# First routing's clearings behind the first gathers, warming matmuls and smaller blocks in it, and the networks' turns, low parts and builds in other slots

## The chip, the cores and the metric

One core of a Trainium2 chip runs the whole program. The metric is the device time of one execution in microseconds (us): 639.29 us is the median of three runs of the kernel before (638.78 to 642.51). The engines are TensorE (PE, matrix products), VectorE (DVE), ScalarE (ACT), GpSimd (POOL) and the transfer queues, of which SyncE's (SP) carries weights and clearings and POOL's the indirect gathers and scatters. Each engine works through its own instructions in order and waits on the others by semaphores.

## The reference

Three stages follow one another, on 24,576 rows (tokens) of 256 values:

```python
X = np.fft.fft(np.fft.fft(x, axis=1), axis=2).real          # x: 8 x 3072 x 256
# first mixture: E = 8 experts, F = 1024
P = np.exp(x @ w_gate - (x @ w_gate).max())
for _ in range(8):
    P /= P.sum(1, keepdims=True) + 1e-09
    P /= P.sum(0, keepdims=True) + 1e-09
    P *= N / E
out = sum(P[:, e:e + 1] * (np.maximum(x @ w1[e], 0) @ w2[e]) for e in range(E))
# second mixture: only the expert with the largest logit, times its softmax probability
expert_idx = np.argmax(logits, axis=1)
out2[mask_e] = gate_w[mask_e, None] * (np.maximum(x[mask_e] @ u1[e], 0) @ u2[e])
```

## The kernel before

The kernel computes the transform (`fft_phase`, to about 196 us), stores the half spectrum in a table `H` (a row and its mirror share an entry; even and odd parts lie side by side), and then works on the rows that carry weight. The **first routing** (`route1`, L575) finds those rows: it makes a list of 29 tiles of 128 slots (24 for the experts, CAP = 3 each, and NF1 = 5 free ones). The position of each row in the list comes out of one-hot matmuls. DVE builds blocks of one-hot columns `ah` (`rows`, L556) of the sizes in CH1 = (24, 24, 16), and PE multiplies each column with 58 columns of `bv` (`runs`, L568, the matmul in L572). From the sums in PSUM (`pt`) DVE makes the row numbers `Rhidx`, POOL gathers rows of `H` into `Xg` (`grab`, L1366, one indirect transfer per tile, with two small clearings of `grow` ahead of each from group 2 on), and a second small product, `bq` against the first block, gives positions in the accumulator. Meanwhile PE has matmuls for the gates of the second mixture (`gates2`, L1279); the string table G2 (L1497) says, one string for each of seven places in the routing, what is put there: "g" one gate piece of 16 matmuls, "0" to "3" low parts, "l" the load of `Ld`, "z" six clearings of the result (`zeros(2)`, 512 KB each from the zero tile `zt`) and the accumulator's clearing (L1348), "v" two warming matmuls on a zero tile `zb`. The clearings are issued on SP.

Each of the eight expert **networks** is computed with weights and activations split in two parts, high and low (`part`, L836: the high part on ACT, the low, `w1l`, `w2l`, on DVE in 1.22 us), three products per block: eight blocks of the first layer (L916, `ph`), `hh` by ACT (L902) and the low part `hl` by DVE (L438), and then the second layer (L949, `py`) in three tiles of slots. So PE waits for `hl` wherever DVE is occupied. Other work is hung into that order by hand. `Slots` has places (e, s) of expert e: s = 0 to 7 behind the first-layer blocks, 8 to 10 the free tile, 11 the turn, 12 to 20 in the second layer's three tiles. Tables say where it goes: PART low and high parts of the next expert's weights, BUILD and FBUILD the four steps in which a gathered group becomes input `x` (add, sign, add, subtract, in `build`, L1620), GRAB1 the gathers, LOGIT the logits of a group, PROB the probabilities of the second mixture, STEPS the eight Sinkhorn rounds. In a round the column sum goes through PE (L1022, `cs`) and ACT (L1023, `total`); the rest is a chain of small DVE operations (`turn`): scale the columns, sum the rows, reciprocal, scale, mask, column sum.

`route1` also returns `later`, the rest of the routing (the free tiles' expert, nine DVE operations: `nf` to `Rfrow`), which `moe1` runs at slot (0,4) in `begin`. The second routing and the second network (`route2`, `moe2`) are built alike; their `later` runs ahead of the second network.

Of the kernel before, what the change touches and what calls it, by code (L numbers as in the profile page):

```python
# [7 lines left out]
F32 = mybir.dt.float32  # L8
# [362 lines left out]
CH1, CH2 = (24, 24, 16), (10, 10, 9)  # L371
# [75 lines left out]
class Route:  # L447
# [9 lines left out]
    def positions(self, T, M, n, rst, nf_, hook=lambda: None, S=None, n1=None, between=()):  # L457
# [56 lines left out]
        def later():  # L514
# [5 lines left out]
            s1, s2 = R["sel"][:, :nf_], S([nf_, 8], name="s2_")  # L520
# [4 lines left out]
            ef = S([nf_], name="ef")  # L525
            o.red(ef, s2, ALU.add)
            wr = S([nf_], name="wr")
# [28 lines left out]
    def rows(self, pool, rb, a, n):  # L556
        m = self.K["irx"].shape[2]
        ah = pool(128 * m)[:, :128 * n].rearrange("p (r i) -> p r i", i=n)
        self.o.tt(ah, self.K["irx"][:, :, :n], rb[:, None, a:a + n].to_broadcast([128, 128, n]), ALU.is_equal)
        return ah  # L560
# [14 lines left out]
def route1(nc, rt, L, rmx, K, R, keep, pool, ring, hooks):  # L575
# [4 lines left out]
    S = lambda sh, dt=F32, name=None: keep.tile([128] + list(sh), dt, name=name)  # L580

# [77 lines left out]
    gp, later = rt.positions(T, M, NSA, C("rst"), NF1, during, S, NSL)  # L659
# [23 lines left out]
    eq, gq = T([8, NSL], name="eq"), T([8], name="gq")  # L683
    lst, li = S([2, NT1], name="lst"), T([NT1], I32, name="li")
# [10 lines left out]
    def signs():  # L695

        o.cp(lst, pv)
# [3 lines left out]
        o.ts(R["valid"], lst[:, 0], 0.5, ALU.is_ge)  # L701
        o.ts(sf, lst[:, 1], 127.5, ALU.is_ge)
        o.stt(R["prim"], sf, -1.0, R["valid"], ALU.mult, ALU.add)
        o.stt(R["ow"], R["hidx"], 2.0, sb, ALU.mult, ALU.add)

        o.tt(eq, ja[:, NSL:NSL + 8, None].to_broadcast([128, 8, NSL]), ja[:, None, :NSL].to_broadcast([128, 8, NSL]), ALU.is_equal)
        o.tt(eq, eq, gp[:, None, :NSL].to_broadcast([128, 8, NSL]), ALU.mult)
        o.red(gq, eq, ALU.add)
        tq, rq, _ = rt.split(T, gq, None, 8, "q")
# [11 lines left out]
        rt.more()  # L721
        pq = rt.py.tile([128, 512], F32, name="py")
        rt.runs(pq, late, bq, 0, 24, True, True)
        st["pq"] = pq

    def targets():

        lq = R["lq"]
# [22 lines left out]
def route2(nc, rt, lg, K, R, pool, ring, arrive, more, counts, warm):  # L751
# [3 lines left out]
    T = lambda sh, dt=F32, name=None: pool.tile([128] + list(sh), dt, name=name)  # L755
    mx, km, rk, kp = T([NT1], name="mx"), T([NT1], name="km"), T([NT1, 8], name="rk"), T([NT1], name="kp")
# [34 lines left out]
    gp, later = rt.positions(T, M, NT1, C("rst2"), NF2, during, between=at)  # L791
# [187 lines left out]
def sinkhorn(nc, K, R, pt, pool):  # L979
# [31 lines left out]
    def rows(it):  # L1011
# [3 lines left out]
        V.reciprocal(ri, rs)  # L1015
        o.tt(P, P, bc(ri), ALU.mult)
# [29 lines left out]
    for it in range(8):  # L1046
        steps += [turn(it), sums]
# [125 lines left out]
def run(tc, ctx, A, out, H, acc, Ld, Pd, Gd, Zd):  # L1173
# [19 lines left out]
    for nm, sh, dt in (("gm", [1], F32), ("ovf", [1], F32), ("sel", [max(NF1, NF2), 8], F32), ("hidx", [NT1], I32),  # L1193
                       ("sg", [NT1], F32), ("valid", [NT1], F32), ("prim", [NT1], F32), ("apos", [E], I32), ("oidx", [NF1], I32), ("lq", [2, E], F32),
# [41 lines left out]
    with tc.manual_schedule():  # L1236
# [27 lines left out]
        with ExitStack() as st:  # L1264
# [50 lines left out]
            with ExitStack() as s1:  # L1315
                r1 = P(s1, "r1", 1, side="right")
                r1a = P(s1, "r1a", 3, side="right")
                ring = lambda n: r1a.tile([128, n], BF16, name="ah")
# [13 lines left out]
                def fill(k):  # L1332

                    def f():
                        for c in G2[k]:
# [5 lines left out]
                            elif c == "z":  # L1341
                                for _ in range(6):
                                    zeros(2)
# [19 lines left out]
                signs, later = route1(nc, rt, L, rmx, K, R, S, r1, ring, [fill(i) for i in range(1, 5)] + [lambda: low(0, 1)])  # L1363
# [14 lines left out]
                for j in (0, 1):  # L1378
                    grab(j)
                fill(5)()  # L1380
                signs()
                fill(6)()
                assert not half
                warm(W2)
            with ExitStack() as s1:
# [4 lines left out]
                def rest():  # L1390
                    later[2]()
# [504 lines left out]
```

## Time and profile before

| what | value |
|---|---|
| median of three runs | 639.29 us |
| profiled execution, its time | 638.99 us |
| its span | 637.2 us |
| PE busy | 615.2 us (97%) |
| DVE busy | 435.4 us (68%) |
| ACT busy | 328.6 us (52%) |
| POOL busy | 194.1 us (30%) |

The span runs from the first to the last instruction; the execution's time holds 1.8 us more around it. Rows of a timeline give the start of a group of like instructions, how long the group takes, its engine and line, what it writes and reads, and in brackets the idle time ahead of it and what ended that. Where matmuls follow each other, their ends are modelled, so that rows of neighbours overlap. [...]

### The profile page before, as it was taken

What the parts mean: (1) busy time and instruction counts of PE and PEld (TensorE: products, weight loads), DVE (VectorE), ACT (ScalarE), POOL (GpSimd) and SP (SyncE); (2) the same over time, 40 slices, a digit from 0 to 9 for tenths busy, and PEclk for the clock granted to TensorE, in tenths of its full rate; (3) what the DMA queues carried; (4) which work ended last, traced back from release to release, by engine and by line L of the source; (5) the groups of instructions that cost most, each with busy time, mean ns of one, the idle gap of its engine ahead of it and who ended that gap; (6) DMA issues with size and microseconds to landing.
All of it is one profiled execution on the core that took longest, in us unless ns stands there. A gap on an engine that the chain in (4) does not pass through costs nothing. (4 is left out here: it accounts for less than half of the span.)

```text
span 637.2 us, 12627 instructions
## 1 busy us (share of the span) xinstructions
PE 615.2 (97%) x4778; PEld 593.4 (93%) x4783; DVE 435.4 (68%) x981; ACT 328.6 (52%) x756; POOL 194.1 (30%) x318
## 2 busy tenths in 40 slices
PE   9999999999999999999999999999999999999995
PEld 6889999999999998999899999986899999999995
DVE  3697877688346977759898796856755664754760
ACT  3455555555544504547566468642455564654551
POOL 0002201221011058871201101223785655422422
PEclk9999999999999958999999999999999999999998
DMA  8999999999998976787877989863655548436421
GB/s 211 284 247 273 275 274 285 279 264 296 341 338 246 414 274 223 221 304 258 281 238 289 338 299 239 196 179 61 224 181 190 197 160 308 184 137 275 175 83 38
DMA packets 56927, 152.56 MB, mean 239 GB/s; under 512 B 8307, under 2 KB 25851, under 8 KB 49436
## 3 DMA queue, kind: packets, MB, share of 16 engines
q1 hardware_dynamic: 47644, 114.69, 58.2%
q0 software_dynamic: 8752, 36.50, 16.8%
q8 instruction: 39, 0.64, 0.4%
q10 hardware_dynamic: 464, 0.51, 0.2%
q14 instruction: 28, 0.23, 0.1%
HBM read 101.50 MB, written 50.07 MB: 238 GB/s over the span
## 5 line engine op out<-in xcount | busy, mean ns | idle before, releaser
L438 DVE SCALAR_TENSOR_TENSOR hl<-ph,hh 128x384 fp32r<-128x384 f32 (+1 forms) x161 | 85.1, 543 | 78.0 <-ACT hh L902 77.8
L949 PE MATMUL py<-w2h,hh 128*128 128x256 f32 (+1 forms) x472 | 136.0, 288 | 0.9 <-ACT lg L1678 0.9
L949 PE MATMUL py<-w2h,hl 128*128 128x256 f32 (+1 forms) x472 | 133.7, 283 | 1.1 <-DVE hl L438 1.0
L949 PE MATMUL py<-w2l,hh 128*128 128x256 f32 (+1 forms) x472 | 133.1, 282 | 0.3 <-DVE w2l L854 0.3
L902 ACT ACTIVATE hh<-ph 128x384 fp32r<-128x384 f32 (+1 forms) x161 | 75.9, 481 | 57.4 <-PE ph L916 33.9
L949 PEld LDWEIGHTS py<-w2h,hl 128*128 128x128 f32 x472 | 88.8, 188 | 1.9 <-DVE hl L438 1.9
L949 PEld LDWEIGHTS py<-w2h,hh 128*128 128x128 f32 x472 | 88.9, 188 | 1.5 <-ACT lg L1678 1.3
L949 PEld LDWEIGHTS py<-w2l,hh 128*128 128x128 f32 x472 | 89.1, 189 | 0.5 <-DVE w2l L854 0.5
L916 PE MATMUL ph<-xh,w1h 128*128 128x384 f32 x256 | 68.2, 347 | 4.0 <-DVE hl L438 3.2
L916 PE MATMUL ph<-xh,w1l 128*128 128x384 f32 x256 | 65.8, 339 | 0.0
L916 PE MATMUL ph<-xl,w1h 128*128 128x384 f32 x256 | 65.6, 338 | 0.0
L823 POOL DMA_INDIRECT out_dram<-y,Rorow x30 | 34.8, 1159 | 86.4 <-ACT hh L902 43.7
L126 POOL TENSOR_TENSOR lc<-hd 128x32 f32<-128x32 f32 x23 | 9.0, 393 | 164.5 <-ACT hd L122 150.5
L74 PE MATMUL pp<-ca,w 96*128 96x96 f32 x512 | 59.0, 275 | 0.0
L74 PEld LDWEIGHTS pp<-ca,w 96*128 96x128 f32 x512 | 58.2, 192 | 0.5 <-ACT Z L97 0.2
L916 PEld LDWEIGHTS ph<-xh,w1h 128*128 128x128 f32 x256 | 45.4, 190 | 6.6 <-DVE hl L438 4.8
L84 DVE COPY t<-pp 128x512 f32<-128x512 f32 (+2 forms) x56 | 33.3, 609 | 23.9 <-PE pp L82 23.9
L91 PE MATMUL pp<-cb,t 128*128 128x128 f32 x368 | 47.5, 276 | 0.6 <-DVE t L84 0.6
L916 PEld LDWEIGHTS ph<-xh,w1l 128*128 128x128 f32 x256 | 46.9, 190 | 0.0
L76 ACT ACTIVATE at<-pp 128x384 f32<-128x384 f32 x64 | 31.0, 490 | 30.6 <-PE pp L74 30.1
L916 PEld LDWEIGHTS ph<-xl,w1h 128*128 128x128 f32 x256 | 46.7, 190 | 0.0
L91 PEld LDWEIGHTS pp<-cb,t 128*128 128x128 f32 x368 | 44.4, 192 | 0.9 <-DVE t L84 0.8
(346 smaller groups left out, 1251.0 us busy)
## 6 DMA issues: line engine op xcount, KB each, us to landing
out_dram<-zt SPq DMA_DIRECT2D x48, 512.0 KB, 7.2
H<-hd SPq DMA_DIRECT2D x24, 562.0 KB, 10.2
xa<-in_xa_dram SPq DMA_DIRECT2D x32, 384.0 KB, 11.1
xm<-in_xm_dram SPq DMA_DIRECT2D x32, 384.0 KB, 8.7
rawa<-in_w_dram SPq DMA_DIRECT2D x8, 1024.0 KB, 8.2
rawb<-in_w_dram SPq DMA_DIRECT2D x8, 1024.0 KB, 5.1
rawa<-in_u_dram SPq DMA_DIRECT2D x8, 1024.0 KB, 8.9
rawb<-in_u_dram SPq DMA_DIRECT2D x8, 1024.0 KB
```

The source lines that it names most:

```text
L74: nc.tensor.matmul(p[:M, i], lhs(4 * h + i), ca, start=True, stop=True)
L76: nc.scalar.activation(out=at[:M, :, :, s0:s0 + 4], in_=p[:M].rearrange("m s g j -> m g j s"), func=AF.Copy)
L84: nc.vector.tensor_copy(out=t[:, :n, :M], in_=p[:, :n, :M])
L91: nc.tensor.matmul(p[:M, i * 128:(i + 1) * 128], t[:, i, :M], cb[:, (g0 + i) * 128:(g0 + i + 1) * 128], start=True, stop=True)
L126: eng.tensor_tensor(out=lc[:np_, :n], in0=hd[:np_, :, 129:137], in1=hd[:np_, :, 273:281], op=ALU.add)
L438: self.nc.vector.scalar_tensor_tensor(out, a, s, b, op0, op1)
L823: nc.gpsimd.indirect_dma_start(out=dst, out_offset=bass.IndirectOffsetOnAxis(ap=idx, axis=0), in_=src, in_offset=None, **kw)
L902: self.nc.scalar.activation(out=a[:, :n], in_=p[:, :n], func=AF.Relu)
L916: self.nc.tensor.matmul(p[:, :N], w, xx, start=(i == 0), stop=(i == 5))
L949: self.nc.tensor.matmul(p[:, :nd], c, W[2 + m // 4][w][:, m % 4, :nd], start=(m == 0 and i == 0), stop=(m == 7 and i == 2))
```

## The change

**First routing.** The string with "z" loses five of its six clearings (the letter is now "a": one `zeros(2)` and the accumulator's clearing). The five stand on SP behind a small memset of `zt` on POOL that follows the gathers of group 0, so they start when those have been issued. Four warming matmuls on `zb` stand behind the first block's 24, and the blocks are of 24, 16, 16 and 8 columns. The low part of the first expert's `w1` (1.22 us on DVE) and several small operations (valid, sf, prim, Row) go behind the slot list and `signs`; two products (`eq`) go ahead of it. The build of each of the first three rows has the sign folded into the add and the subtract (`pair`, with `sg` and its negative `ng`), with the copy of two columns on ACT.

**Later.** The nine operations of the routing's rest go from slot (0,4) to (0,18); the second network's from ahead of it to (0,12).

**Networks.** The tables BUILD, FBUILD, LOGIT, PROB and STEPS name other slots. A Sinkhorn round is cut in three steps (turn, shares, sums) where it was two; the second low part of a free tile's weights goes behind the `hl` of slot (e,2). In the second network the `behind` list goes from (0,0) to (0,1), `part("u",0,3)` from (0,1) to (0,3), and the gather of the free tile's weights from ahead of the X gathers to (0,14).

```diff
-CH1, CH2 = (24, 24, 16), (10, 10, 9)
+CH1, CH2 = (24, 16, 16, 8), (10, 10, 9)
...
     for n in CH1:
         ah = rt.rows(ring, rb, a, n)
-        if late is None:
+        first = late is None
+        if first:
             late = ah
             spans(0, GL, "p")
             hooks[3]()
         rt.runs(pl, ah, bv, a, n, a == NSL, a + n == NSL)
+        if first:
+            hooks[4]()
         a = (a + n) % NSA
-    hooks[4]()
...
-                for j in (0, 1):
-                    grab(j)
-                fill(5)()
-                signs()
-                fill(6)()
+                grab(0)
+
+                nc.gpsimd.memset(zt[:, 0, 0:8], 0.0)
+                for _ in range(5):
+                    zeros(2)
+                grab(1)
+                fill(6)()
+                signs()
+                low(0, 1)
+                fill(7)()
...
+        def pair(g, c):
+            o.stt(x[j][:, i, c], X[j][:, i, 137:264], g[:, CAP * j + i:CAP * j + i + 1], X[j][:, i, 2:129], ALU.mult, ALU.add)
...
     for it in range(8):
-        steps += [turn(it), sums]
+        steps += [turn(it), shares, sums]
...
-BUILD = ((0, (5, 6, 6, 6)), (1, (0, 1, 2, 3)), (2, (1, 2, 3, 4)), (2, (12, 13, 14, 16)), (3, (12, 13, 14, 16)), (5, (0, 1, 2, 3)), (5, (12, 13, 14, 16)))
+BUILD = ((0, (6, 6, 11, 12)), (1, (0, 0, 1, 2)), (2, (1, 2, 6, 7)), (2, (12, 13, 14, 16)), (3, (12, 13, 14, 16)), (5, (0, 1, 2, 3)), (6, (1, 1, 2, 4)))
-FBUILD = ((1, (4, 6, 6, 7)), (4, (1, 2, 3, 4)))
+FBUILD = ((1, (5, 6, 7, 12)), (4, (1, 2, 3, 4)))
-G2 = ("g", "", "ggggggg", "0lg1zg2g3", "gg", "gg", "g")
+G2 = ("g", "", "ggggggg", "0lg1ag2g3", "gg", "vv", "gg", "g")
-    for i, f in zip((0, 1, 2, 3, 4), (lambda: rest[3](1, 1), rest[0], lambda: rest[3](1), rest[1], begin)):
+    for i, f in zip((0, 1, 2, 3, 4, 18), (lambda: rest[3](1, 1), rest[0], lambda: rest[3](1), rest[1], begin, rest[5])):
```

Three places show how the instructions stand on their engines.

**SP and POOL, first routing.** SP's queue at the end of the transform and after it, of the kernel before; `zt` is the zero tile, `out_dram` the result, `acc` the accumulator, `Ld`, `Gd` and `rawa` are loads.

```order
L1340 DMA Ld<-L 128x1552
L1210 DMA out_dram<-zt 128x2x512 x6
L1348 DMA acc<-zt 128x512 x3
L1348 DMA acc<-zt 128x54
L1292 DMA Gd<-g_76 128x8x64
L1233 DMA rawa<-in_w_dram 128x2048
```

The same place of the changed kernel:

```order
L1350 DMA Ld<-L 128x1552
L1220 DMA out_dram<-zt 128x2x512
L1357 DMA acc<-zt 128x512 x3
L1357 DMA acc<-zt 128x54
L1220 DMA out_dram<-zt 128x2x512 x5
L1302 DMA Gd<-g_76 128x8x64
L1243 DMA rawa<-in_w_dram 128x2048
```

Five clearings of 512 KB have moved behind the accumulator's, and in front of the stores of `Gd` and the next weights' load. POOL's order there, first before:

```order
L818 DMA Xg<-H,Rhidx 128x281 x6
L1375 MEMSET grow 8x256 x2
L818 DMA Xg<-H,Rhidx 128x281
L1375 MEMSET grow 8x256 x2
L818 DMA Xg<-H,Rhidx 128x281
```

and of the changed kernel:

```order
L826 DMA Xg<-H,Rhidx 128x281 x3
L1389 MEMSET zt 128x8
L826 DMA Xg<-H,Rhidx 128x281 x3
L1384 MEMSET grow 8x256 x2
L826 DMA Xg<-H,Rhidx 128x281
```

The memset of `zt`, for which the five clearings wait, stands between the gathers of group 0 and those of group 1; nothing else of POOL's order moves here.

**DVE, the slot list.** The last one-hot blocks (`ah`), the list's row numbers (`j`, `li`, `hr`, `pp`, `Rhidx`) and what follows, of the kernel before:

```order
L429 TENSOR_TENSOR ah<-irx,rba 128x3072
L429 TENSOR_TENSOR ah<-irx,rba 128x2048
L852 TENSOR_TENSOR w1l<-rawa,w1h 128x1024
L435 TENSOR_SCALAR j<-pt 128x29
L441 CAST li<-pt 128x29
L435 TENSOR_SCALAR hr<-j 128x29
L433 TENSOR_SCALAR pp<-li 128x29
L429 ISA Rhidx<-hr,pp 128x58
L441 COPY lst<-pt 128x58
L433 TENSOR_SCALAR sb<-j 128x29
L435 TENSOR_SCALAR Rsg<-sb 128x29
L433 TENSOR_SCALAR Rvalid<-lst 128x29
```

and of the changed kernel:

```order
L429 TENSOR_TENSOR ah<-irx,rba 128x2048 x2
L429 TENSOR_TENSOR ah<-irx,rba 128x1024
L429 TENSOR_TENSOR eq<-ja 128x320
L429 TENSOR_TENSOR eq<-eq,gsa 128x320
L435 TENSOR_SCALAR j<-pt 128x29
L441 CAST li<-pt 128x29
L435 TENSOR_SCALAR hr<-j 128x29
L433 TENSOR_SCALAR pp<-li 128x29
L429 ISA Rhidx<-hr,pp 128x58
L433 TENSOR_SCALAR sb<-j 128x29
L435 TENSOR_SCALAR Rsg<-sb 128x29
L444 TENSOR_REDUCE gq<-eq 128x8
```

`w1l` has left this stretch, and the two products of `eq`, which stood four rows below the last row shown of before, stand where it stood; `lst`, `Rvalid` and its neighbours no longer stand between `Rhidx` and `gq`.

**DVE, start of the fourth expert.** A Sinkhorn turn and the `hl` of the first-layer blocks, before:

```order
L435 TENSOR_SCALAR cs<-total 128x8
L1027 RECIPROCAL cs<-cs 128x8
L429 TENSOR_TENSOR P<-P,cs 128x29x8
L444 TENSOR_REDUCE rs<-P 128x29
L1015 RECIPROCAL ri<-rs 128x29
L429 TENSOR_TENSOR P<-P,ri 128x29x8
L429 TENSOR_TENSOR P<-P,Rprim 128x8x8
L444 TENSOR_REDUCE cs<-P 128x8
L438 SCALAR_TENSOR_TENSOR hl<-ph,hh 128x384 x2
```

and of the changed kernel:

```order
L435 TENSOR_SCALAR cs<-total 128x8
L1037 RECIPROCAL cs<-cs 128x8
L429 TENSOR_TENSOR P<-P,cs 128x29x8
L444 TENSOR_REDUCE rs<-P 128x29
L1023 RECIPROCAL ri<-rs 128x29
L438 SCALAR_TENSOR_TENSOR hl<-ph,hh 128x384 x2
L438 SCALAR_TENSOR_TENSOR hl<-ph,hh 128x256
L438 SCALAR_TENSOR_TENSOR hl<-ph,hh 128x384 x2
L429 TENSOR_TENSOR P<-P,ri 128x29x8
L429 TENSOR_TENSOR P<-P,Rprim 128x8x8
L444 TENSOR_REDUCE cs<-P 128x8
```

Five `hl` steps stand between the first five operations of the turn and its last three.

## Rows read from the trace of the kernel before

**Rows 1.** Head of the profile's page, whole program.

```profile
span 637.2 us, 12627 instructions
```

**Rows 2.** Timeline, PE, 219 to 246: start, duration, instruction [idle before, releaser].

```profile
219.09 1.95 PE L1279 MATMUL py<-wg,rawc 128*128 128x96 f32 x16
221.14 1.84 PE L572 MATMUL pt<-bv,ah 128*128 128x58 bf16 x24
224.28 2.88 PE L572 MATMUL pt<-bv,ah 128*128 128x58 bf16 x40 [1.29 <-DVE ah L429]
226.98 3.71 PE L1279 MATMUL py<-wg,rawc 128*128 128x96 f32 x16
...
240.91 1.07 PE L916 MATMUL ph<-xh,w1h 128*128 128x384 f32 x2 [0.37 <-ACT xh L872]
...
244.33 0.56 PE L916 MATMUL ph<-xl,w1h 128*128 128x384 f32 x2
```

**Rows 3.** Windows of 2 us: busy time by engine, granted clock, DMA share.

```profile
224.00:226.00 2.00, 1.72 (x25) 1.73 (x26) 2.00 (x3) 0.00 (x0) 0.00 (x0) 0.50 1.05 408
```

**Rows 4.** Waits of PE, 250 to 460: total us, times, longest.

```profile
PE ph L916 <- DVE hl L438: 3.2, 5, 1.0
PE py L949 <- DVE hl L438: 1.0, 2, 0.8
PE py L949 <- ACT lg L1678: 0.9, 2, 0.7
PE pt L1022 <- DVE cs L444: 0.5, 1, 0.5
...
PE pt L896 <- ACT total L1023: 0.3, 1, 0.3
...
PE py L949 <- DVE w2l L854: 0.3, 1, 0.3
```

**Rows 5.** Timeline, PE, first layer of expert 3.

```profile
311.66 0.51 PE L916 MATMUL ph<-xl,w1h 128*128 128x384 f32 x2
313.18 0.61 PE L916 MATMUL ph<-xh,w1h 128*128 128x384 f32 x2 [1.00 <-DVE hl L438]
```

**Rows 6.** Timeline, PE, warming matmuls of the second routing.

```profile
436.16 3.20 PE L1298 MATMUL py<-zb 128*128 128x512 bf16 x13
```

**Rows 7.** Timeline, DVE, first routing and first row build.

```profile
222.47 2.89 DVE L429 TENSOR_TENSOR ah<-irx,rba 128x3072 bf16<-128x3072 bf16 x2
...
227.73 0.19 DVE L429 CUSTOM_DVE_ANT_0 Rhidx<-hr,pp 128x58 uint16<-128x58 uint16 x1
...
234.20 0.30 DVE L1622 TENSOR_TENSOR Xg<-Xg 128x33 f32<-128x33 f32 x2 [1.54 <-DMA Xg<-H,Rhidx]
...
236.60 0.49 DVE L1622 TENSOR_TENSOR x<-Xg 128x127 f32<-128x127 f32 x2
```

**Rows 8.** Timeline, POOL, gathers of row groups 0 and 6.

```profile
230.97 0.95 POOL L818 DMA_INDIRECT Xg<-H,Rhidx  x1 [0.30 <-issue]
...
271.89 1.36 POOL L818 DMA_INDIRECT Xg<-H,Rhidx  x1 [0.16 <-issue]
```

**Rows 9.** Timeline, SP's queue, clearings ahead of the first routing.

```profile
210.50 10.67 SPq L1210 DMA_DIRECT2D out_dram<-zt  x6
```

**Rows 10.** Line L818 (gathers), issued 228.3 to 231.5: landing times.

```profile
DMA to landing us min/median/max: 3.9/4.9/6.0
```

**Rows 11.** The same line, issued 235 to 239.4.

```profile
DMA to landing us min/median/max: 3.0/3.0/3.0
```

**Rows 12.** Timeline, DVE, experts 0 and 1.

```profile
251.09 0.14 DVE L433 TENSOR_SCALAR nf<-inb 128x1 f32<-128x1 f32 x1
...
252.59 0.19 DVE L441 CAST Rfrow<-wr 128x5 int32<-128x5 f32 x1
...
279.88 0.17 DVE L429 TENSOR_TENSOR sg__3039<-Xg 128x24 f32<-128x24 f32 x1
```

**Rows 13.** Line L818 again, issued 261 to 272.

```profile
DMA to landing us min/median/max: 4.3/6.6/8.5
```

More of the change, by code (lines that the diff above doesn't have):

```diff
@@ L580, in route1 @@
     S = lambda sh, dt=F32, name=None: keep.tile([128] + list(sh), dt, name=name)
+    Q = lambda sh, dt=F32, name=None: stay.tile([128] + list(sh), dt, name=name)
     m1 = S([1], name="m1")
@@ L721, in signs @@
         rt.more()
+        o.stt(R["ow"], R["hidx"], 2.0, sb, ALU.mult, ALU.add)
         pq = rt.py.tile([128, 512], F32, name="py")
@@ L724, in signs, with kinds @@
         st["pq"] = pq
+    def kinds():
+        o.ts(R["valid"], lst[:, 0], 0.5, ALU.is_ge)
+        o.ts(sf, lst[:, 1], 127.5, ALU.is_ge)
+        o.stt(R["prim"], sf, -1.0, R["valid"], ALU.mult, ALU.add)
     def targets():
+        kinds()
         lq = R["lq"]
@@ L748, in route1, with route2 @@
     return signs, (targets, overflow, later)
-def route2(nc, rt, lg, K, R, pool, ring, arrive, more, counts, warm):
+def route2(nc, rt, lg, K, R, stay, pool, ring, arrive, more, counts, warm):
     o = rt.o
@@ L755, in route2 @@
     T = lambda sh, dt=F32, name=None: pool.tile([128] + list(sh), dt, name=name)
+    S = lambda sh, dt=F32, name=None: stay.tile([128] + list(sh), dt, name=name)
     mx, km, rk, kp = T([NT1], name="mx"), T([NT1], name="km"), T([NT1, 8], name="rk"), T([NT1], name="kp")
@@ L790, in route2 @@
     more(counts[2])
-    gp, later = rt.positions(T, M, NT1, C("rst2"), NF2, during, between=at)
+    gp, later = rt.positions(T, M, NT1, C("rst2"), NF2, during, S, between=at)
     tb, rb, _ = rt.split(T, gp, (cs, ca), NT1, "b", tp)
@@ L1361, in low @@
                     del lows[k][:n]
-                signs, later = route1(nc, rt, L, rmx, K, R, S, r1, ring, [fill(i) for i in range(1, 5)] + [lambda: low(0, 1)])
+                signs, later = route1(nc, rt, L, rmx, K, R, S, kp, r1, ring, [fill(i) for i in range(1, 6)])
                 X = {}
@@ L1400, in ask @@
                     zeros(2)
-                turned, more = moe1(nc, K, R, rt, lg, hot, acc, moe, W, part, X, xg, Gd, *rows("w1", "w2"), xb, pt, zeros, zt, later[:2] + (rest, low, grab), ask, rt.C("tro"), lambda i: None, lambda: xg.tile([128, CAP, HW], F32, name="Xg").rearrange("p a b -> p (a b)")[:8, :512])
+                turned, more = moe1(nc, K, R, rt, lg, hot, acc, moe, W, part, X, xg, Gd, *rows("w1", "w2"), xb, pt, zeros, zt, later[:2] + (rest, low, grab, later[2]), ask, rt.C("tro"), lambda i: None, lambda: xg.tile([128, CAP, HW], F32, name="Xg").rearrange("p a b -> p (a b)")[:8, :512])
             with ExitStack() as s1:
@@ L1430, in arrive @@
                     choose(0, NT1)
-                later = route2(nc, rt, lg, K, R, r2, ring, arrive, more, Y2, lambda: warm(W3))
+                later = route2(nc, rt, lg, K, R, kp, r2, ring, arrive, more, Y2, lambda: warm(W3))
                 def grab2(j):
@@ L1462, in run @@
                 yb = P(s1, "yb2", 4)
-                moe2(nc, R, out, moe, W, part, X, xg, *rows("u1", "u2"), yb, check, grab2, xt, behind)
+                moe2(nc, R, out, moe, W, part, X, xg, *rows("u1", "u2"), yb, check, grab2, xt, behind, later)
     flag = nc.values_load(fi[0:1, 0:1], min_val=0, max_val=1)
@@ L1530, in experts @@
         if 0 <= f < n:
+            behind = [] if s == "w" else None
+            if s == "w":
+                sl.at(e, 2, lambda b=behind: b.pop()())
             for i in (4, 5):
[L1532 removed]
+                sl.at(e + at[i] // 21, at[i] % 21, lambda f=f, i=i, g=g, b=behind if i == 5 else None: free.part(f, i - 2, g(i), b))
     for e in range(E):
@@ L1800, in moe1, with moe2 @@
     return q, more
-def moe2(nc, R, out, moe, W, part, X, xg, w1f, w2f, yb, check, grab, xt, behind):
+def moe2(nc, R, out, moe, W, part, X, xg, w1f, w2f, yb, check, grab, xt, behind, later):
     o = Ops(nc)
@@ L1833, in moe2 @@
     sl.at(1, 3, check)
-    sl.at(0, 0, *behind)
-    sl.at(0, 1, lambda: part("u", 0, 3, V))
-    free.weights(0)
+    sl.at(0, 1, *behind)
+    sl.at(0, 3, lambda: part("u", 0, 3, V))
+    sl.at(0, 12, later)
+    sl.at(0, 14, lambda: free.weights(0))
     for j in (E, 2, 3):
```

53 lines of the change are left out of this document (25 added, 28 removed).

## Prediction

> **What bounds the kernel now.** I read the head of the profile's page first: the profiled execution's span is 637.2 us [rows 1], and TensorE (PE) is busy in 97% of it, so PE's order of work is the chain and a microsecond is won only where PE waits, runs at half clock, or does work that can go. So I looked for those places in PE's timeline and asked for the granted clock in short windows.
>
> They are of two kinds. The first is the first routing, 219 to 245 us. [...] What PE did before the fall: a block of 24 small matmuls (L572, 58 columns), then 1.29 us of idle until VectorE (DVE) had built the next one-hot block [rows 2]. The half clock lasts until about 244.4: the first network's pair at 240.91 takes 1.07 us, the one at 244.33 only 0.56 [rows 2]. The second kind are short waits of the network stage: 3.2 us in five waits of first-layer matmuls for `hl`, 1.0 for `hl` in the second layer, 0.9 for `lg` on ScalarE (ACT), 0.5 for the column sums, 0.3 for ACT's `total` and 0.3 for `w2l` [rows 4]. A wait costs more than its bracket: the pair before the 1.00 us wait starts at 311.66, a pair's starts are 0.34 apart at full clock (half of the 0.68 that five pairs in 3.42 us give at half clock, below), so the next was due at 312.00 and came at 313.18: 1.18 us [rows 5]. I add 0.16 to each bracket.
>
> **The change part by part.** *Slot list.* Block 1's 24 matmuls end at 222.98 [rows 2]. Behind them PE now finds four warming matmuls of 512 columns. Thirteen such take 3.20 us elsewhere [rows 6], starts about 0.22 apart, so four fill 0.86 us, to 223.84, of the 1.29 us gap. The two later one-hot blocks took DVE 2.89 us for 40 columns from 222.47 [rows 7], 0.072 a column; the first 16 columns are there at 223.6, the next at 224.8, the last 8 at 225.4, so PE runs its 40 matmuls (2.88 us [rows 2]) without a wait to 226.72, where it was 227.16: 0.44 earlier. `Rhidx` ended at 227.92 [rows 7] and should at 227.48; two products of the later `eq` step (0.5 us each) go into the DVE idle time ahead of it.
>
> *Gathers.* The third gather started at 230.97 [rows 8] and so at 230.53 now. Before, 3 MB of clearings (six transfers, 10.67 us of the queue [rows 9]) and the accumulator's were still moving; the first three gathers landed 6.0, 4.9 and 3.9 us after issue [rows 10], the next three, with the clearings out, 3.0 each [rows 11]. With five of the six clearings behind them I take 2.96: third row at 233.49, where it was 234.89. [...]
>
> *Row build.* Five DVE operations of a row took from 234.20 on 0.93 us a row, three rows to 237.1 [rows 7]. Two of them become one each with the sign folded in and the copy goes to ACT: about 0.75, so the last row ends at 234.25.
>
> *PE up to the network.* From 226.72 two gate pieces at full clock, 3.6 us (twice 1.95 less the row's tail): 230.3. `bq` needs some 1.7 us less ahead of it on DVE (two `eq`, three kind operations, 1.22 of `w1l` later): ready at about 230.6. Its 24 matmuls take 1.7 (0.072 each, as the block matmuls do at half clock, 40 in 2.88 us, and at full, 24 in 1.84: their rate is not the clock's) to 232.3, one gate piece 1.8 to 234.1, the three transposes to 234.6, ACT's `xh` and the start 0.7: first network matmul at **235.3, where it is 240.91 [rows 2]: −5.6**. Of this the clock carries most: the gates alone are halved from 10.4 us to 5.4.
>
> *Network start.* From 240.91 to 244.33 ten instructions take 3.42 us [rows 2] and at full clock half, −1.7. The low part `w1l` now follows the row builds (1.22 us) and holds the second half up to about 236.7, +0.6. **−1.1.**
>
> *Waits.* Nine operations of the routing's rest ran on DVE from 251.09 to 252.78 [rows 12], ahead of the `hl` for which PE waited 0.17 and 0.84 us; they are in slot (0,18) now, a second-layer slot, where only `hl` of expert 0's end stands near. Their second copy leaves the start of the second network. The Sinkhorn turn is cut in two, three of its operations (1.2 us) behind a step of `hl`, and low parts and builds go to later slots. The waits reached: all of `hl` (4.2), the larger `lg` 0.7, 0.5, 0.3 and 0.3: 6.0 in brackets, eleven of them, plus 0.16 × 12 (one is counted from its neighbours): **7.9**. No operation vanishes from DVE; the cover is DVE's idle time between `hl` steps, and DVE is 68% busy. Where it fails, the wait returns in another slot. Stays: I take 1.2.
>
> *What is late next.* POOL's order is hardly changed, and it gives its gathers one at a time behind two small clearings. PE is some 9 us ahead of its old time, the gathers are not. The third gather of group 6 starts at 271.89 [rows 8] and those of its stretch land 4.3 to 8.5 us later [rows 13]; it would be used for the logits before 279.88 [rows 12], which now stand at about 271: DVE waits some 4 us there, with `hl` operations behind it. PE runs on what is ready; I take 1.5 us lost, 0.7 for group 8: **+2.2**. Bounds: 0 if DVE's slack covers it, 4 if all of it reaches PE. Waits on zt: POOL's memset must wait for the accumulator's clearing to be read; it stands behind the first three gathers, so only the others wait, and those have 3 us in hand.
>
> **Sum.** −5.6 −1.1 −7.9 +1.2 +2.2 = −11.2. Against the profiled execution of 638.99 (span 637.2 and 1.8 around it), 627.8; the median of the runs is 0.3 above it: **628.0**.
>
> **Rivals.** A, as above, 628.0. B, the clock falls later: the `bq` matmuls (16 columns, PE hardly loaded) or the wait for the third gather come right ahead of the network, and half clock there costs up to 1.7 us of network, 1.8 of gate and half of the transposes: about +3, **630.9**. For it: before, the fall came behind small matmuls and idle. Against: gates stand on both sides of `bq`. C, the clock falls where it fell before, since the 40 small matmuls follow the four warmings as they followed the idle time: the gates and the start are again at half, and of the 6.7 us only 1.9 stay (0.44 from the slot list, 1.4 from the earlier rows), **632.8**. D, the waits move rather than go, or group 6 to 8 hold PE by 4 us more: **631.8**. For it: DVE 68% busy in full stretches, the chain of low parts as it is. E, the third gather lands 3.9 us after its issue as before, since the one clearing that stays ahead and the weights' loads are enough to slow it: the first network starts 0.9 us later than in A, **628.9**. F, the other side: POOL's memset waits for SP's clearing transfers that read zt, and with them all later gathers. It decides from about 245 us on, when group 1's rows must be there, that is if the memset is held 12 us or more; every microsecond beyond it is one of PE, and 24 us of hold would give 12 lost, **640**. Against: the last clearing ahead of it is issued some 9 us earlier than before, so it should be out at about the third gather's time.
>
> **How the numbers follow.** Chances: A 0.44, B 0.24, C 0.14, D 0.11, E 0.04, F 0.03. Prediction 628.0. The range reaches over B and D to C's price and, below, takes in all waits gone and no late gathers (−3.4): **624.6 to 633.0**. A measurement of this kernel can tell about 1%, here 6.4 us, from no change; its border is 632.9. Faster by more: A, B, D, E and a third of C, 0.87; within: the rest of C, 0.10; slower by over 1%: 0.03, from F.
>
> **What would show it.** Clock 1.00 through 224 to 244 (A) or a new fall and its place (B, C); gates in 1.95 us a sixteen; landing of the first three gathers about 3 us (not 3.9 to 6); the first L916 at 235.3; no `hl` wait of over 0.2 us in experts 0 to 5, and none at the second network's start; the DVE waits for the group 6 to 8 gathers, and whether a PE wait stands beside them. Wrong would be: clock 0.50 anywhere between the blocks and the network, waits on `hl` at new slots, POOL idle behind the memset.

## The result and the profile after

The changed kernel takes 644.05 us (median of 20 runs, 640.79 to 647.2) where the kernel before takes 639.5 (20 runs beside them): a ratio of 1.0058, 95% interval 1.0042 to 1.0074. So it is slower, and 16 us above the forecast. Its profiled execution takes 643.69 us. From the head of its page: the span, the busy time of the engines, and the granted clock of PE in 40 slices (tenths of full speed; the windows further down give it as a share, and half clock is 0.50), which answer [rows 1]:

```profile
span 641.9 us, 12659 instructions
PE 616.7 (96%) x4787; PEld 594.7 (93%) x4787; DVE 433.9 (68%) x977; ACT 329.3 (51%) x759; POOL 198.1 (31%) x319
PEclk9898999999999997999999899999999999999998
```

PE waits more than before, not less: 641.9 − 616.7 is 25.2 us without a matmul, before 22.0. PE's timeline through the first routing, for [rows 2] (start, duration, instruction, idle before and what ended it):

```profile
223.84 1.87 PE L572 MATMUL pt<-bv,ah 128*128 128x58 bf16 x24
225.54 1.03 PE L1361 MATMUL ph<-zb 128*128 128x512 bf16 x4
226.44 2.83 PE L572 MATMUL pt<-bv,ah 128*128 128x58 bf16 x40
229.11 2.00 PE L1289 MATMUL py<-wg,rawc 128*128 128x96 f32 x16
...
235.99 0.39 PE L1289 MATMUL py<-wg,w1l 128*128 128x96 f32 x2
242.29 1.54 PE L877 MATMUL pt<-ident,x 128*128 128x128 f32 x6 [5.92 <-issue]
244.20 1.07 PE L924 MATMUL ph<-xh,w1h 128*128 128x384 f32 x2 [0.37 <-issue]
```

Up to the last gate matmul all is as forecast: the warming matmuls fill the gap, the gates run sixteen in 2.00 us (3.71 before), and from 223.84 to 235.99 are 12.2 us. Then PE stands still for 5.92 us ahead of the first transposes. Windows of the same trace (busy time of PE, PEld, DVE, ACT, POOL; granted clock; DMA share; GB/s), for [rows 3]:

```profile
224.00:226.00 2.00, 2.00 (x27) 1.76 (x27) 1.97 (x3) 1.43 (x3) 0.00 (x0) 1.00 1.05 399
...
236.50:242.00 5.50, 0.00 (x0) 0.00 (x0) 1.93 (x5) 0.07 (x1) 4.71 (x10) 0.65 1.04 383
...
246.00:248.00 2.00, 2.00 (x8) 2.00 (x8) 0.89 (x2) 0.49 (x1) 1.78 (x4) 0.50 1.05 390
```

The clock is 1.00 where it was 0.50 before (224 to 226), but falls to 0.50 at 238.1, in the hold, and stays there for 10.2 us, into the first network. ACT's timeline shows what the transposes wait for:

```profile
233.81 0.20 ACT L1291 ACTIVATE g<-py 128x32 f32<-128x32 f32 x1 [2.46 <-PE py L1289]
241.94 0.20 ACT L1291 ACTIVATE g<-py 128x32 f32<-128x32 f32 x1 [7.93 <-remote]
242.03 0.39 ACT L1655 ACTIVATE x<-Xg 128x2 f32<-128x2 f32 x3
```

The three copies of two columns (L1655), which the change gave to ACT, stand behind the copy of the last gate piece, and that runs at 241.94, 5.6 us after its last matmul ended (235.99 and 0.39). PE's waits of the network stage, 250 to 470 (total us, times, longest), for [rows 4]:

```profile
PE pt L1032 <- DVE cs L444: 2.0, 1, 2.0
PE pt L1032 <- DVE xl L429: 2.0, 1, 2.0
PE pt L904 <- DVE Xg L1637: 1.1, 1, 1.1
...
PE py L957 <- ACT y L1848: 0.7, 1, 0.7
```

The waits for `hl` are nearly gone (0.4 us are left of 4.2), and others of the same sum stand at the Sinkhorn sums (L1032), at the free tile's turn (L904) and in the second network.

A ledger by stage, from PE's timeline of each trace, in us. "Start" is the first one-hot block matmul (ahead of it stand the transform and the first steps of the routing), "routing" reaches from it to the first network's first matmul, "first" from there to the second network's, "second" to its last. In the last column, stretches at half clock up to there: start, length. "Before, again" and "after, on another chip" are the runs b1 and c1 below.

| execution | start | routing | first | second | half clock, us |
|---|---|---|---|---|---|
| before, the profile read | 221.14 | 19.77 | 207.48 | 181.27 | 223.9: 20.5 |
| forecast | 221.1 | 14.2 | 201.9 | 181.3 | none |
| after | 223.84 | 20.36 | 209.45 | 181.35 | 16: 3.4, 47: 6.8, 238.1: 10.2, 357.6: 3.4 |
| before, again | 223.82 | 16.62 | 206.62 | 180.75 | 16: 3.4, 47: 6.8, 227.8: 6.8 |
| after, on another chip | 224.07 | 14.54 | 207.44 | 181.37 | 17: 3.4, 47: 6.8 |

The kernel before stands here twice, and so does the changed one. So three questions stood open: what the hold of 5.92 us is, what the routing is worth without it, and where the 5.6 us went that the forecast takes off the first network (207.5 to 201.9).

### The profile page after: what moved, and what is told of

It reads as the page before. It is cut to its first block, busy times and chain, and to the rows that moved or that the text cites. A ratio compares the mean times of both kernels' runs of the same rounds, so it can differ in the third digit from the quotient of the medians.

```text
span 641.9 us, 12659 instructions
## 1 busy us (share of the span) xinstructions
PE 616.7 (96%) x4787; PEld 594.7 (93%) x4787; DVE 433.9 (68%) x977; ACT 329.3 (51%) x759; POOL 198.1 (31%) x319
## 5 line engine op out<-in xcount | busy, mean ns | idle before, releaser
L74 PE MATMUL pp<-ca,w 96*128 96x96 f32 x512 | 62.0, 283 | 0.0
L74 PEld LDWEIGHTS pp<-ca,w 96*128 96x128 f32 x512 | 61.3, 200 | 0.8 <-issue 0.3
```

The source lines that it names most:

```text
L74: nc.tensor.matmul(p[:M, i], lhs(4 * h + i), ca, start=True, stop=True)
```

## The experiments

Each ratio is against the kernel before on the same chip. Edits are to the changed kernel where nothing else is said.

**Clearings and copies.** The hold could come from the five clearings, which now move beside it, or from the copies on ACT. One kernel puts the clearings back (and drops the memset), one only the copies, one puts the clearings into slots of the second expert.

```
x1   -  zeros(2)
     +  for _ in range(6): zeros(2)
     -  nc.gpsimd.memset(zt[:, 0, 0:8], 0.0); for _ in range(5): zeros(2)
x2   -  nc.scalar.activation(out=x[j][:, t, 0:2], in_=X[j][:, t, 0:2], func=AF.Copy)
     +  eng.tensor_copy(out=x[j][:, t, 0:2], in_=X[j][:, t, 0:2])
x4   -  ZERO = [(), (16, 19), ...]
     +  ZERO = [(), (12, 13, 14, 15, 16, 18, 19), ...]
     -  nc.gpsimd.memset(zt[:, 0, 0:8], 0.0); for _ in range(5): zeros(2)
```

> The changed kernel with one thing undone: all six clearings stand again ahead of the accumulator's clearing on SP, and the small memset of zt is gone. In the changed kernel ACT's copy of the last gate piece, and behind it the transposes of the first network, began 5.5 to 5.9 us after their inputs were there, in the time in which the five moved clearings went out. Theory C (the moved clearings cause the hold): no hold here; the third gather lands about 3.9 us after its issue as before, the first network starts some 15.5 us after the first one-hot block's matmuls (19.8 in the kernel before, 20.4 in the changed one), total about 639.2 us. Rival A (the hold comes of the new chain PE, ACT copy, PE, whatever the transfers do): hold of 5 us or more stays, about 644 to 645 us.

> The changed kernel with the three two-column copies of the first row build on DVE again, as before the change, so that the transposes no longer wait for ACT. Theory C (the moved clearings hold back ACT's work): transposes start at once, but ACT's xh still stands behind the held gate copy, first network as late as in the changed kernel, about 644 us. Rival A (the new chain through ACT makes the hold): hold gone, first network some 14.5 us after the first block's matmuls, about 638.5 us.

> The changed kernel with the five clearings in slots of the second expert's second layer (12, 13, 14, 15, 18) instead of behind the first gathers, and without the memset of zt. Theory C: no hold, the three gathers land about 3 us after their issue, the first network starts some 14.5 us after the first block's matmuls, the clock stays at 1.00 or falls for less long, total about 638 us; later clearings may slow gathers there by up to 2 us. Rival A (the chain through ACT): hold of 5 us or more stays, about 644 us.

Measured: x1 639.26 against 638.25 (1.002, 0.9992 to 1.0049), x2 636.26 (0.9968, 0.9947 to 0.9989), x4 637.49 (0.9989, 0.9962 to 1.0016). None of the three has the hold: their routings take 15.51, 14.75 and 14.78 us. That looked like three proofs, and was none, since the changed kernel itself had not yet run on that chip. It then ran on another, without any edit (c1):

> The changed kernel itself once more. The routing part alone held exactly its routing instructions, moved clearings and ACT copies included, and showed no hold, while the changed kernel's profile had one of 5.9 us. Theory H (the hold belongs to the changed kernel): a hold of 5 us or more between the last gate piece and the transposes again, time 0.5% over the kernel before. Rival R (the hold was of that one stretch of runs, not of the kernel): no hold, first network some 12.5 us after the first block's matmuls, time as with the copies on DVE, about 0.3% under the kernel before (636 where it takes 638).

It took 638.27 against 637.57 (1.0013, 0.9989 to 1.0038), with the same clearings and the same copies, and no hold. ACT's timeline of this run, with the copies of the last two gate pieces, then PE's:

```profile
233.18 0.20 ACT L1291 ACTIVATE g<-py 128x32 f32<-128x32 f32 x1 [1.59 <-PE py L1289]
236.66 0.20 ACT L1291 ACTIVATE g<-py 128x32 f32<-128x32 f32 x1 [3.28 <-PE py L1289]
236.75 0.58 ACT L1655 ACTIVATE x<-Xg 128x2 f32<-128x2 f32 x3
```

```profile
236.23 0.39 PE L1289 MATMUL py<-wg,w1l 128*128 128x96 f32 x2
237.01 1.23 PE L877 MATMUL pt<-ident,x 128*128 128x128 f32 x6 [0.39 <-ACT x L1655]
238.61 0.83 PE L924 MATMUL ph<-xh,w1h 128*128 128x384 f32 x2 [0.38 <-ACT xh L880]
```

The last gate copy runs 0.04 us after its last matmul, and the network starts 14.54 us after the first block. One thing x1 does tell: what the moved clearings are worth in the routing. Landing times of its first three gathers, min, median and max, and below them those of c1:

```profile
DMA to landing us min/median/max: 3.7/4.5/5.6
```

```profile
DMA to landing us min/median/max: 2.9/3.4/3.9
```

With the clearings ahead, as before [rows 10], PE does its transposes row by row, and the network starts 0.7 to 0.8 us later than in x4 and x2 on the same chip, 1.0 later than in c1. The moved clearings then slow the next five gathers: they land 5.9 to 6.2 us after issue in c1, and with a median of 5.9 in x2, where x1, on x2's chip, has 3.5.

**The routing alone and the networks alone.** x3 keeps the routing's edits and takes the tables, the steps of a turn, the place of `later` and the second network's order from before; c2 is before with those.

> The routing part of the change alone: tables, Sinkhorn steps, later and the second network's order as in the kernel before. Theory N (the networks' part of the change gained nothing, its waits moved to the column sums, the free tile's turn and the inputs' builds, and with a fall of the clock it cost about 2 us): about 642 us, the network stage from its first matmul to the second network's as long as before (207.5 us). Rival (the networks' part gained some 4 us net and the routing alone lost more than 8): about 648 us.

> The networks' part of the change alone (tables, split Sinkhorn round, later, second network's order), routing as in the kernel before. Theory N (the waits moved and did not go): PE's excess between 250 and 460 us about as large as before (some 8 us, now at the column sums of rounds 3 and 6, the free tile's turn, a y or lg), time within 0.3% of the kernel before. Rival (the networks' part gains its 6 to 7 us where the gathers are not late): 0.8 to 1% faster than before, 632 where it takes 638.

x3: 636.23 against 638.25, 0.9965 (0.9944 to 0.9986), routing 14.77. c2: 639.63 against 637.57, 1.0023 (1.0004 to 1.0042), first network 206.18. So the routing brings 2.0 us, and the networks' part brings nothing: by the medians it costs 2.1 us, by the interval of the ratio 0.3 to 2.7. Its waits, when the listed rows are added up over 250 to 470, are 8.5 us (two of 2.0 at the sums among them) against 8.0 of the kernel before in the run below.

**Before, run again.** Both runs have nearly the same ledger, unlike the profile that I forecast from.

> The kernel before itself, for a second profile of it. The prediction took its 20.5 us at half clock from one execution; the networks' part alone, with the same routing, had only 6.8 us at half clock there, and 10.2 us at half clock in the transform, where the profiled execution of before had none. Theory V (the profiled execution was not typical: the fall in the routing is usually shorter, and the transform has one of its own): half clock in the routing 7 to 10 us, routing up to the first network 17 us instead of 19.8, block 1 starting at 224 instead of 221. Rival (a long fall is the rule): 20 us again.

> The kernel before once more, a third profile, for the same question: theory V 7 to 10 us at half clock in the routing and 17 us up to the first network, rival 20 us and 19.8 us.

636.45 and 636.86 us. Windows of the first:

```profile
16.00:18.00 2.00, 2.00 (x11) 1.72 (x12) 1.91 (x3) 0.73 (x2) 0.00 (x0) 0.55 1.04 279
...
48.00:52.00 4.00, 4.00 (x20) 4.00 (x20) 3.01 (x4) 1.23 (x3) 0.00 (x0) 0.50 0.77 188
```

```profile
226.00:228.00 2.00, 1.04 (x15) 1.05 (x16) 2.00 (x3) 0.00 (x0) 0.00 (x0) 0.96 1.05 408
228.00:230.00 2.00, 2.00 (x30) 2.00 (x29) 1.29 (x4) 0.00 (x0) 0.00 (x0) 0.50 1.05 406
...
236.00:238.00 2.00, 2.00 (x27) 2.00 (x27) 1.91 (x12) 0.07 (x1) 1.48 (x2) 1.00 0.40 103
```

The same gap behind the first block, the same fall behind it, but only 6.8 us at half clock where the profile read had 20.5; the clock is back within PE's second gate piece, and the network starts at 240.44, 16.62 us after the first block. In return this execution has falls in the transform, at 16 and 47 us, which the profile read had not, and its blocks start 2.7 us later.

**The sums.** In the changed kernel the sums of rounds 3 and 6 wait 2.0 us each. DVE's timeline ahead of the first:

```profile
323.96 0.49 DVE L438 SCALAR_TENSOR_TENSOR hl<-ph,hh 128x384 fp32r<-128x384 f32 x1
324.37 1.21 DVE L860 TENSOR_TENSOR w2l<-rawb,w2h 128x1024 fp32r<-128x1024 f32 x1
325.50 0.18 DVE L862 TENSOR_TENSOR w2l<-g,w2h 128x32 fp32r<-128x32 f32 x1
325.60 0.55 DVE L438 SCALAR_TENSOR_TENSOR hl<-ph,hh 128x384 fp32r<-128x384 f32 x1
326.07 0.39 DVE L429 TENSOR_TENSOR P<-P,ri 128x232 f32<-128x232 f32 x1
326.50 0.23 DVE L429 TENSOR_TENSOR P<-P,Rprim 128x64 f32<-128x64 f32 x1
326.76 0.56 DVE L444 TENSOR_REDUCE cs<-P 128x8 f32<-128x232 f32 x1
```

and PE's, which has nothing left ahead of the sum from 325.4 on:

```profile
325.09 0.28 PE L957 MATMUL py<-w2h,hl 128*128 128x264 f32 x1
327.38 0.39 PE L1032 MATMUL pt<-cs,tri 128*128 128x8 f32 x2 [2.00 <-DVE cs L444]
```

The split put the last three operations of this turn behind two `hl` and a low part (1.21 and 0.18 us), and the sum on PE stayed in its slot. The cheap mend is to put the sums two slots later, and the turns behind them with them (c3):

```
-STEPS = [..., 19, 23, 24, 25, ..., 41, 47, 48, 50, 54, 54, 56, 62, 63]
+STEPS = [..., 19, 25, 26, 27, ..., 41, 49, 50, 52, 55, 55, 57, 62, 63]
```

> The changed kernel with the column sums of Sinkhorn rounds 3 and 6 two slots later (and the turns behind them). Theory S (each of the two 2.0 us waits is only a sum put ahead of DVE's last three operations): both waits gone, about 4 us less than the changed kernel run beside it. Rival (DVE is behind altogether, so the wait goes with the slot or comes at the next sum): less than 1 us.

It fell: 638.64 against 637.57, 1.002 (1.0001 to 1.004). PE's timeline of c3, then DVE's:

```profile
322.46 0.49 PE L1032 MATMUL pt<-cs,tri 128*128 128x8 f32 x2 [2.32 <-DVE xl L429]
...
323.18 0.42 PE L957 MATMUL py<-w2l,hh 128*128 128x264 f32 x1
323.40 0.42 PE L957 MATMUL py<-w2h,hl 128*128 128x264 f32 x1
```

```profile
319.77 0.57 DVE L444 TENSOR_REDUCE cs<-P 128x8 f32<-128x232 f32 x1
...
320.73 1.21 DVE L860 TENSOR_TENSOR w1l<-rawa,w1h 128x1024 fp32r<-128x1024 f32 x1
321.86 1.01 DVE L429 TENSOR_TENSOR xl<-pt,xh 128x384 fp32r<-128x384 f32 x2
```

`cs` is ready at 320.34 and PE still waits until 322.46: now for `xl`, which reads the PSUM tile `pt` that the sum is to overwrite, and which stands behind a `w1l`. The second wait of the changed kernel, of 1.95 us at 357.35, is of the same kind (its row names `xl`). So the slot of a sum is bounded on both sides: behind its turn, and ahead of the next transposes in `pt`, whose reader is late. The turn itself has to come earlier. c4 keeps c3's sums and mends the other waits (free tile's build back, logits of groups 6 and 7 to (2,3) and (2,7), the second network's `later` to (0,17) and weights' gather to (0,18), copies on DVE); c5 is c4 with the turns of rounds 3 and 6 whole again and their sums where they were:

```
c5 against c4
-STEPS = [3, 4, 5, 11, 12, 14, 17, 17, 19, 25, 26, 27, 31, 32, 35, 39, 39, 41, 49, 50, 52, 55, 55, 57, 62, 63]
+STEPS = [3, 4, 5, 11, 12, 14, 17, 17, 17, 23, 24, 25, 31, 32, 35, 39, 39, 39, 48, 48, 50, 54, 54, 56, 62, 63]
```

> The changed kernel with its new waits taken out one by one: the two sums two slots later, the free group's build in the slots of before, the logits of groups 6 and 7 in slots (2,3) and (2,7) so that no hl stands behind a late gather, the second network's nine operations at (0,17) behind its probabilities, the three small copies on DVE. Theory: waits of 2.0, 1.95, 1.1, 0.7 and up to 1.3 us gone, about 6 to 7 us less than the changed kernel run beside it without a hold, 629 to 631 where the kernel before takes 638. Rival (what is mended comes back elsewhere): 634 or more.

> The kernel with the waits mended, but with the column sums of rounds 3 and 6 where the kernel before has them and these two turns whole again (the last three operations right behind the first five). Theory P (in the changed kernel the sum of round 3 waited because the split put the last three operations behind two low parts, and that of round 6, and both sums when put two slots later, because the product's PSUM tile waits for xl of the next expert's turn): both waits gone, an hl wait of up to 1.2 us back in the fourth expert, 3 us less than the kernel with the sums two slots later, about 632 where the kernel before takes 637.6. Rival (DVE is behind, any order waits): within 1 us of it.

c4: 634.99 against 637.57, 0.9977 (0.9955 to 0.9999). c5: 631.53 against 637.28, **0.9898 (0.9867 to 0.9929)**, faster than both kernels. From PE's timeline of c5:

```profile
348.73 0.39 PE L1032 MATMUL pt<-cs,tri 128*128 128x8 f32 x2 [0.93 <-DVE xl L429]
```

Of the sums' waits one of 0.93 is left, the listed waits over 250 to 470 are 5.0 us together (8.9 in the changed kernel), and the first network takes 204.16 where c4's takes 206.97.

**Later and the logits alone.** c6 is x3 with `later` at (0,18), the first BUILD row of the change, and the logits of groups 6 and 7 six and five slots later:

```
-LOGIT = (..., (1, 5), (1, 12), (1, 18), (2, 2), (0, 16), (2, 7))
+LOGIT = (..., (1, 5), (1, 12), (2, 3), (2, 7), (0, 16), (2, 7))
```

> The routing part alone, plus the two changes of the network stage that only fill idle DVE time: the nine operations at (0,18) with the first build in (0,6) to (0,12), and the logits of groups 6 and 7 behind the first hl of their expert. Theory: the waits of 1.1, 0.3, 1.0 us in the first expert and 1.1 us in the third go, 3.5 us less than the routing alone: about 633 where the kernel before takes 638 (0.992). Rival (they come back elsewhere, as they did in the changed kernel): 635.5 or more.

634.07 against 637.28, 0.9946 (0.9924 to 0.9968); the first network takes 205.40 where x3's takes 208.12. The waits of expert 0 (0.90, 0.17 and 0.83 us in x3) are gone, and the one at group 6's logits is 0.45 where it was 0.97. How late those gathers are, DVE's timeline of x2 shows:

```profile
283.48 0.18 DVE L429 TENSOR_TENSOR sg__3034<-Xg 128x24 f32<-128x24 f32 x1 [6.58 <-DMA Xg<-H,Rhidx]
```

**The hold again.** Three more runs of the changed kernel itself on one chip, then one on another with two of the mended kernels beside it, to separate clearings from copies where the hold shows:

> The changed kernel a third time. In its first profile ACT's copy of the last gate piece ran 5.5 us after the piece's last matmul and PE stood 5.9 us; in the second profile, and in three kernels with the same routing, there was none. Theory H2 (the hold is a rare event of some executions, with any moved clearing): a profile in several shows it, the time spreads by 5 us, median between 0 and 0.6% over the kernel before. Rival R (it belonged to the first stretch of runs): none here, time about 0.1% over the kernel before, 638 to its 637.5.

> The changed kernel a fourth time, one look: H2 a hold of 5 us in some profiles, R none; the network stages as in the second profile (207.4 and 181.4 us), the routing 14.5 us.

> The changed kernel a fifth time, one look: H2 a hold of 5 us in some profiles, R none; the network stages as in the second profile (207.4 and 181.4 us), the routing 14.5 us.

> The changed kernel once more, as the measure for the two kernels beside it: four of its five profiles had a hold of 4.6 to 7.3 us between the last gate piece and the transposes, one on another chip had none. Theory H3 (it depends on the chip): either all profiles of this call that keep the cause show it, or none does.

> The changed kernel with the five clearings in slots of the second expert instead of behind the first gathers, beside the changed kernel on the same chip. If the changed kernel is held here: theory C (the clearings in flight beside the gathers make the hold) no hold and 4 to 6 us less than it; rival A (the chain PE, ACT copy, PE makes it) a hold as long. If the changed kernel is not held here: the same time as it within 2 us, and the question stays open.

> The changed kernel with the three small copies on DVE, beside the changed kernel on the same chip. If the changed kernel is held here: theory C a hold as long, now seen at ACT's xh, since the gate's copy stands ahead of it; rival A no hold and 4 to 6 us less. If the changed kernel is not held here: the question stays open.

d1 to d3 took 644.71, 646.32 and 644.45 us against 639.62 (the first timed: 1.0081, 1.0051 to 1.0111); all three have the hold (4.55, 7.33 and 5.96 us of PE). From ACT's and PE's timelines of d1:

```profile
240.77 0.20 ACT L1291 ACTIVATE g<-py 128x32 f32<-128x32 f32 x1 [6.55 <-remote]
```

```profile
241.12 1.54 PE L877 MATMUL pt<-ident,x 128*128 128x128 f32 x6 [4.55 <-ACT g L1291]
```

On the other chip the changed kernel (638.46 against 638.14) does not show it, so the kernels beside it (f2, which is x4, 0.9991, 0.9974 to 1.0008; f3, which is x2, 0.9981, 0.995 to 1.0011) tell nothing of it. The hold stands in four of six profiles of one and the same program: in the first, whose chip isn't known, and in the three of d1's chip; it is in neither of the two on other chips (c1, f0). On a chip that shows it, neither the clearings elsewhere nor the copies on DVE were tried.

The held traces themselves say something of both suspects, for ACT is late one copy earlier. In the first profile the last matmul of the gate piece before the last, then SP's clearings:

```profile
232.51 0.39 PE L1289 MATMUL py<-wg,w1l 128*128 128x96 f32 x2
```

```profile
234.11 4.62 SPq L1220 DMA_DIRECT2D out_dram<-zt  x5
```

The copy of that piece was due at 232.9 and ran at 233.81 (its row stands in the first section): 0.91 us late, and still ahead of the first moved clearing. In d1, d2 and d3 it is 0.90, 0.91 and 0.24 us late, each time ahead of that clearing's issue; in the kernel before, in x1 to x4 and in c1 each of these copies runs 0.03 to 0.05 us behind its last matmul. So the five clearings did not start the lateness, though they may lengthen it, and the copies of two columns stand behind the gate copy in ACT's order: they pass the hold on and do not make it.

What else can be said: in the four profiles ACT's last gate copy comes 4.2 to 7.0 us after its matmuls; in the first it ends, at 242.14, before the five clearings do (1,280 packets of 2 KB, the last at 243.6), while the DMA engines are busy throughout (share 1.04 in the window above, but 1.00 also from 236 to 242 in c1, without it); the loads of the page's two instruction queues (q8 and q14, one each) fall at 230 to 236 us with it (the four) and without it (c1, f0); and the first profile holds 7,627 semaphore records where that of the kernel before holds 8,364 (52 against 219 from 230 to 240 us, the time of the first gathers), and its row of that copy, like those of d1 to d3, names only "remote", so that who released ACT can't be read. Whether the missing records and the hold come from one thing is not shown. **Its cause is open.**

## Why the prediction was wrong, step by step

Against the forecast the profiled execution is 15.9 us long (643.69 to 627.8): up to the blocks +2.7, the routing +6.2, the first network +7.6, the second +0.1, the end −0.7. The experiments give a second split, by medians on the same chip: the routing's part was to bring 6.7 us (−5.6 and −1.1) and brought 2.0 (x3), the networks' part was to bring 4.5 (−7.9, +1.2 and +2.2) and cost 2.1 (c2). That is 11.3 of the 16 us, and it agrees with the changed kernel where it isn't held (+0.7, c1). The rest, between 4 and 5 us, comes where the hold is. So without the hold the change is worth nothing, and with it the kernel is slower.

**What bounds the kernel** was right: PE's order is the chain, and where experiments took waits away (c5, c6) the first network became shorter (204.16 and 205.40 against 206.62).

**Slot list, gathers, row build, gates up to the network: right.** Without the hold the routing takes 14.2 to 15.2 us in eleven executions that have the smaller blocks, the warming and the row build (with the clearings behind or elsewhere), forecast 14.2, at their lower end; between the blocks and the network the granted clock is 1.00 in the windows of c1 and x3, and the gates run sixteen in 2.00 us in x2 and x4 too. The first three gathers land in 2.9 to 4.0 us in c1 and x2; I took 2.96 for the third, and the 0.9 us for the clearings were 0.7 to 1.0 (x1).

**The price of the half clock: the term was mis-sized.** The −5.6 and −1.1 us stood against one execution with 20.5 us at half clock. In a further execution of the same kernel (b1) it was 6.8 us (b2 has the same mean granted clock, 0.983), the routing took 16.62, and the gain of the routing is 2.1 us (16.62 to 14.54), by x3's time 2.0. The rest belonged to that execution: it had no half clock ahead of the blocks, where b1 had two stretches (3.4 and 6.8 us) and started the blocks 2.7 us later, so its total was the usual one by another sum. I took the stage from one row and the total from the median, and these did not belong together.

**The hold: a step not seen.** "Three transposes to 234.6" put nothing between gates and transposes. The change had put a new link there: the transposes now wait for ACT, and ACT's copies stand in order behind the gate copy. I costed moving the copy to ACT only by what DVE saves, and named no one queued behind it. Whatever holds the gate copy holds PE, 4.6 to 7.3 us of it in those four executions, and the half clock that comes with it (6.8 us in d1, 10.2 in the first profile) costs more. That ACT's order passes the hold on is what the rows show; what makes the hold, they don't. Nor is the new link shown to matter: ACT's `xh`, for which the network's first matmuls wait, stands behind the same gate copy in both kernels, so a held copy would reach PE without the link too, one step later.

**Waits −7.9, of which +1.2 stay: wrong, and the largest error that experiments settle.** The `hl` waits did go, as forecast (0.4 us are left, 1.0 in c1). "Where it fails, the wait returns in another slot" was the sentence that decided, and I gave it 1.2 us: two waits of 2.0 at the sums, 1.1 at the free tile's turn, 0.7 in the second network came in their place, and the first network gained next to nothing (206.18 in c2, 206.62 and 206.79 in the kernel before). I had counted what a split turn frees (its last three operations, ahead of `hl`), and not who waits for its end: PE's sum, in an unmoved slot. c5 gives that part back: whole turns with their sums in the old slots take the first network from 206.97 (c4) to 204.16, 2.8 us, with no half clock in either (mean granted clock 0.998 in c4; in c5 only two of the 40 slices, both ahead of 63 us, are under nine tenths); the medians, on two chips, differ by 3.5 (634.99 and 631.53). Rival D, at 0.11, was the mechanism; its price of 4 us was too small, for c2 is 6.6 us from the forecast.

**Late gathers +2.2: about right for group 6, wrong in place for group 8.** DVE waits 6.58 us at group 6's logits in x2 and PE about 1 us for it (0.97 in x3). Group 8's 1.1 us came, but ahead of the free tile's turn, whose build the change had put in later slots; it is gone in c4, where the build is back, so I put it down to those slots and not to the landing.

**The rivals.** B's clock fall near the network came in the hold, at 238.1, and not behind `bq`, which ended at 234.5; in c1 and x3, without the hold, the windows up to the network show none. C didn't come. F didn't: the memset runs at 233.95 right behind the third gather, and POOL goes on. The side was wrong since no rival took three things together: a gain of the routing a third as large, the waits moving, and PE held once more.

## What to carry to other kernels

Before a stage is priced by its clock, read a second execution: where the half clock falls is not the kernel's alone (20.5 and 6.8 us of it in the routing of one kernel), and a stage of one execution must not be set against the median of many. When an operation is moved to spare its engine, name who waits for its end, what stands ahead of it on the new engine, and which tile's reader the waiting instruction needs; matmuls of 8 columns waited 1.95 us here for another step's `xl`. And before a mend is credited, run the unmended kernel on the same chip.

## What the runs showed of the hardware that was not expected

**Half clock wanders between executions of the same program.** The kernel before ran at half clock for 20.5 us in one execution and for 6.8 in another (b1) behind the same gap (1.29 and 1.28 us). The stretch ahead of the blocks had two falls (3.4 and 6.8 us, in the first profile of the changed kernel and in b1) or none (in the first of the kernel before), and the blocks started between 221.1 us there and 224.3 in x2. Behind the 2.32 us wait of c3 the clock falls (the second-layer steps 0.22 us apart instead of 0.12); behind the same wait in c4 (2.3 us) it does not: the mean granted clock of that execution is 0.998. Of the changed kernel's two waits at the sums (2.0 and 1.95 us), the second is followed by 3.4 us at half clock in the first profile, and neither in c1. So the falls of the routing and the networks stand in or behind waits of PE here, but waits of one length bring one or none; and ahead of the two falls in the transform (at 16.2 and 47.0 us in the first profile) PE's waits list none in 10 us.

**A hold that came with the chip or the time.** One program was held 4.6 to 7.3 us at one place in three profiles of three on one chip, and in neither of the two taken on other chips, while the kernel before took 637.6 to 639.6 us (medians) on the three. Its times agree: 643.6 to 645.3 us in six runs on the first, 634.0 to 641.4 in twelve on the second. Whether it is the chip or the stretch of time in which it ran was not separated.
